# Padding the sine and cosine tables of a kernel's second Fourier transform, so that each table transfer is one whole tile

## The chip, the core and the metric

The kernel runs on one core of one Trainium2 chip. The metric is the device time of one execution in microseconds (us). An execution that is profiled is one of these, and its trace is what the rows below are taken from.

## What is computed

Causal attention (2 batches, 12 heads, 448 positions, 64 channels per head), then a mixer block over tokens and channels, then a block that adds the real part of a two-dimensional Fourier transform, normalizes, and runs a second two-layer network:

```python
attn_out = _attn_ref(**attn_kwargs)
x = attn_out.transpose(0, 2, 1, 3).reshape(B, S, H * D)      # 2 x 448 x 768
# _moe_ref
h = np.maximum(x.transpose(0, 2, 1) @ w_tok1, 0.0) @ w_tok2
u = x + h.transpose(0, 2, 1)
x = u + np.maximum(u @ w_ch1, 0.0) @ w_ch2
# _moe2_ref
X = np.fft.fft(np.fft.fft(x, axis=1), axis=2)
u = x + np.real(X)
un = (u - mean(u)) / np.sqrt(var(u) + 1e-06)
return u + np.maximum(un @ w_ch1, 0.0) @ w_ch2
```

## The kernel before

Activations are kept channel-major: `resid[ct][b]` is a tile of 128 channels by 448 positions, for 6 channel tiles `ct` and 2 batches `b`. Every product that must be exact to fp32 is made of three TensorE passes: each operand is split into a high part and a low part (`act_h` and `act_l`, `gh` and `gl`, `wh` and `wl`), and the passes are high by high, high by low and low by high. ScalarE makes the high part, VectorE or GpSimd subtracts it to get the low part.

The weights arrive as 64-bit floats. `fetch` (L132) loads a tile `w` from SyncE's queue; `convert_steps` turns it into `wh` and `wl`: an absolute value on ScalarE (L141), two VectorE operations with constants (L143 and L144, TENSOR_SCALAR on `m`), two VectorE operations that merge in `w` (L148 and L152, SCALAR_TENSOR_TENSOR), the copy to `wh` (L159) and the subtraction to `wl` (L161).

Attention and the token mixer are issued in an order written out by hand (the string `ORDER`). Its last words are `U` to `a`: for the channel network's first four chunks of batch 0, `early_up` multiplies `act_h` and `act_l` by the first weights (L226 to L228), `gh` is made by ScalarE (L232) and `gl` by VectorE (L234); then `early_down` (`Y`, L247 to L249) multiplies two channel tiles of the second layer, each of 12 matmuls whose last ones need the fourth chunk's `gl`. Among the last words is also `split_low` (L510): GpSimd makes `act_l` of batch 1, for which ScalarE makes `act_h` (L506) from what VectorE added up (L502). What is written after that hand-made order (the channel network's other chunks and the conversions of their weights) is placed by a scheduler, which may move it up between the words of `ORDER`; so the conversion of the next weights stands on VectorE ahead of the fourth chunk's `gl`.

The two Fourier transforms are matrix products with tables that the host computes (`_fft_constants`): `fa` and `fa0` for the transform over channels, `fb` for the one over positions, each as a high and a low half. The tables are loaded before the channel network begins, by GpSimd's queue (L592): `fah` and `fal` are 128 partitions of 2352 floats, `fah0` one partition of 386, and `fbh` and `fbl` 113 partitions of two rows. A row of `fb` has `2 * NH` = 452 floats in memory; its tile in SBUF has room for `FB` = 464 in each row:

```python
fbh = fc.tile([113, 2, FB], F32R, name="fbh")
fbl = fc.tile([113, 2, FB], F32R, name="fbl")
for t, src in ((fah, fa[0]), ..., (fbh[:, :, : 2 * NH], fb[0]), (fbl[:, :, : 2 * NH], fb[1])):
    pool.dma_start(out=t, in_=src)
```

So the loads of `fbh` and `fbl` fill 452 of each 464 floats. On GpSimd's queue they stand between two groups of `split_low`. The tables are first read by `plane` (L761), far later, and by `mixed_mean` (L745); both index the first `NH` and the next `NH` columns of a row.

Of the kernel before, what the change touches and what calls it, by code (L numbers as in the profile page):

```python
# [19 lines left out]
B, H, S, D = 2, 12, 448, 64  # L20
# [11 lines left out]
NK = 386  # L32
NH = 226
FB = 464
# [66 lines left out]
def fused_kernel(ctx: ExitStack, tc: tile.TileContext, qk, v, w1, w2, wa, wb, wc, wd, fa, fa0, fb, out):  # L101
# [153 lines left out]
    with ExitStack() as actx:  # L255
# [282 lines left out]
        def early_down(x):  # L538
# [5 lines left out]
            s=mix_low, B=channels, b=channels_copy, D=mix_out, d=mix_add, u=split_high, w=split_low, R=load_raw,  # L544
# [41 lines left out]
    fah = fc.tile([128, 3, NF + 384], F32R, name="fah")  # L586
    fal = fc.tile([128, 3, NF + 384], F32R, name="fal")
    fah0 = fc.tile([1, NF], F32R, name="fah0")[:, :NK]
    fbh = fc.tile([113, 2, FB], F32R, name="fbh")
    fbl = fc.tile([113, 2, FB], F32R, name="fbl")  # L590
    for t, src in ((fah, fa[0]), (fal, fa[1]), (fah0, fa0[:, :NK]), (fbh[:, :, : 2 * NH], fb[0]), (fbl[:, :, : 2 * NH], fb[1])):
        pool.dma_start(out=t, in_=src)  # L592

    fp = fctx.enter_context(tc.tile_pool(name="fold", bufs=1))
# [332 lines left out]
def _split(x):  # L927
    h = _round12(x)
    return np.stack([h, _round12(x - h.astype(np.float64))])
# [7 lines left out]
def _fft_constants():  # L937
    c = np.arange(384)[:, None]
    k = np.arange(NF)[None, :]
    cos = np.where((k < 385) & (c > 0), np.cos(2 * np.pi * ((c * k) % DM) / DM), 0.0)  # L940
    sin = np.sin(2 * np.pi * ((c * k[:, :384]) % DM) / DM)
    fa = np.concatenate([cos, sin], axis=1).reshape(3, 128, NF + 384).transpose(1, 0, 2)
    fa0 = np.where(k < 385, 1.0 - 2.0 * (k % 2), 0.0).astype(np.float32)
    s = np.concatenate([np.arange(112), [0], np.arange(112, 225)])[:, None]
    k = np.arange(NH)[None, :]
    fb = np.zeros((226, 2 * NH))
    fb[:, :NH] = np.cos(2 * np.pi * ((s * k) % S) / S)
    s = np.concatenate([np.arange(1, 113), [0], np.arange(113, 224), [0, 0]])[:, None]
    fb[:, NH:] = -np.sin(2 * np.pi * ((s * k) % S) / S)
    fb = fb.reshape(2, 113, 2 * NH).transpose(1, 0, 2)  # L950
    return _split(fa), fa0, _split(fb)


# [38 lines left out]
```

## Time and profile before

| | |
|---|---|
| median of 3 runs | 699.96 us (698.80 to 701.28) |
| the profiled execution | 699.23 us |
| its span, first to last instruction | 697.5 us |
| TensorE busy (PE) | 682.7 us, 98% |
| VectorE busy (DVE) | 538.8 us, 77% |
| ScalarE busy (ACT) | 290.0 us, 42% |
| GpSimd busy (POOL) | 136.6 us, 20% |
| mean granted TensorE clock | 0.994 of full speed |
| chain that ended last | PE 90%, DVE 6%, ACT 1%, DMA 1%, issue 1% |

PE stands for matmuls, PEld for weight loads into the array, POOLq and SPq for the queues from which GpSimd and SyncE start transfers. A time in a row is counted from the start of the span. "Idle before" is the time in which an engine stood still before an instruction, with what ended it. The busy time of an instruction that writes a transfer's orders (DMA_DIRECT2D) is the time that GpSimd spent writing them; the time to landing is that of the transfer itself.

### The profile page before, as it was taken

The page shows a single profiled execution, that of the slowest core. Times are in us where ns is not written, and L with a number is a line of the kernel's source. Part 1 is how long each engine was busy: PE and PEld are TensorE (multiplying, and loading weights), DVE is VectorE, ACT ScalarE, POOL GpSimd, SP SyncE. Part 2 cuts the span into 40 slices and gives each one's busy share as a digit, 9 for nine tenths or more (in the row PEclk, how much of TensorE's full clock was granted, in tenths as well). Part 3 has the DMA queues.
Part 4 walks back from the last instruction along what each step waited for, and adds up shares of the span by engine and source line. Part 5 has one row for each costly group of instructions (what it writes and reads, how often), then busy time and mean ns, then how long its engine had stood idle before and what let it go on. Part 6 is the DMA issues. An engine that isn't in the chain of part 4 may idle for free.

```text
span 697.5 us, 10309 instructions
## 1 busy us (share of the span) xinstructions
PE 682.7 (98%) x3954; PEld 622.9 (89%) x3954; DVE 538.8 (77%) x886; ACT 290.0 (42%) x622; POOL 136.6 (20%) x113
## 2 busy tenths in 40 slices
PE   8999999969999999999999999999999999999997
PEld 6788888959999999997999999999999999999996
DVE  5998787474996884799999898689887898755832
ACT  7978986413333333233545632133432233323200
POOL 3242445480000000030050005822002321000000
PEclk9999999989999999999999999999999999999999
DMA  8233321262443333010204334053332344322311
GB/s 262 70 116 122 103 95 62 91 180 83 153 133 121 121 122 119 19 75 0 88 20 136 121 122 138 14 180 121 122 120 92 137 136 136 106 74 90 111 43 54
DMA packets 27585, 73.39 MB, mean 105 GB/s; under 512 B 9114, under 2 KB 14176, under 8 KB 27168
## 3 DMA queue, kind: packets, MB, share of 16 engines
q1 hardware_dynamic: 19952, 69.48, 30.3%
q0 software_dynamic: 7584, 3.25, 1.8%
q8 instruction: 31, 0.51, 0.3%
q14 instruction: 18, 0.15, 0.1%
HBM read 69.94 MB, written 2.75 MB: 104 GB/s over the span
## 4 chain that ended last, share of the span: by engine, by line
PE 90%; DVE 6%; ACT 1%; DMA 1%; issue 1%; DVEq 0%; ACTq 0%; SPq 0%
PE psum L228 12%; PE psum L226 12%; PE psum L227 12%; PE psum L249 12%; PE psum L247 12%; PE psum L248 12%; PE psum L334 3%; PE psum L402 3%; PE psum L385 3%; PE psum L466 2%; PE psum L497 2%; PE psum L761 1%; DMA w<-in_wb 1%; PE psum L695 1%; DVE m L148 1%; PE psum L484 1%
## 5 line engine op out<-in xcount | busy, mean ns | idle before, releaser
L249 PE MATMUL psum<-gl,wh 128*128 128x448 f32 x432 | 157.6, 365 | 6.2 <-DVE gl L234 6.2
L247 PE MATMUL psum<-gh,wh 128*128 128x448 f32 x432 | 157.7, 365 | 0.0
L248 PE MATMUL psum<-gh,wl 128*128 128x448 f32 x432 | 157.3, 364 | 0.0
L228 PE MATMUL psum<-actl,wh 128*128 128x448 f32 x432 | 156.7, 363 | 0.0
L226 PE MATMUL psum<-acth,wh 128*128 128x448 f32 x432 | 156.5, 362 | 0.0
L227 PE MATMUL psum<-acth,wl 128*128 128x448 f32 x432 | 156.1, 361 | 0.0
L141 ACT ACTIVATE m<-w 128x512 f32<-128x512 f32 (+2 forms) x92 | 71.1, 774 | 122.3 <-DVE wl L161 69.8
L159 ACT CAST wh<-m 128x512 fp32r<-128x512 f32 (+1 forms) x90 | 63.2, 704 | 103.7 <-PE psum L249 64.4
L249 PEld LDWEIGHTS psum<-gl,wh 128*128 128x128 f32 x432 | 81.7, 189 | 12.5 <-DVE gl L234 6.6
L247 PEld LDWEIGHTS psum<-gh,wh 128*128 128x128 f32 x432 | 81.6, 189 | 5.5
L248 PEld LDWEIGHTS psum<-gh,wl 128*128 128x128 f32 x432 | 81.6, 189 | 5.5
L227 PEld LDWEIGHTS psum<-acth,wl 128*128 128x128 f32 x432 | 81.0, 188 | 5.9
L228 PEld LDWEIGHTS psum<-actl,wh 128*128 128x128 f32 x432 | 81.1, 188 | 5.3
L226 PEld LDWEIGHTS psum<-acth,wh 128*128 128x128 f32 x432 | 81.1, 188 | 5.1
L143 DVE TENSOR_SCALAR m<-m 128x512 f32<-128x512 f32 (+2 forms) x92 | 52.7, 572 | 41.5 <-ACT m L141 41.0
L152 DVE SCALAR_TENSOR_TENSOR m<-w,m 128x512 uint32<-128x512 uint32 (+2 forms) x92 | 78.8, 858 | 1.8
L148 DVE SCALAR_TENSOR_TENSOR m<-w,m 128x512 uint32<-128x512 uint32 (+2 forms) x92 | 78.4, 853 | 2.2
L161 DVE TENSOR_TENSOR wl<-m,wh 128x512 fp32r<-128x512 f32 (+1 forms) x84 | 67.9, 809 | 11.6 <-ACT wh L159 11.3
L234 DVE SCALAR_TENSOR_TENSOR gl<-psum,gh 128x448 fp32r<-128x448 f32 x72 | 43.7, 618 | 28.1 <-ACT gh L232 28.1
L232 ACT ACTIVATE gh<-psum 128x448 fp32r<-128x448 f32 x72 | 38.0, 539 | 65.3 <-PE psum L228 65.3
L144 DVE TENSOR_SCALAR m<-m 128x512 uint32<-128x512 uint32 (+2 forms) x92 | 52.2, 568 | 2.6
L372 ACT ACTIVATE p<-psum,nmx 112x112 f32<-112x112 f32 (+3 forms) x96 | 46.7, 510 | 8.6 <-DVE nmx L357 7.5
(160 smaller groups left out, 845.1 us busy)
## 6 DMA issues: line engine op xcount, KB each, us to landing
w<-in_wc SPq DMA_DIRECT2D x24, 768.0 KB, 4.3
w<-in_wd SPq DMA_DIRECT2D x36, 512.0 KB, 3.3
w<-in_wa SPq DMA_DIRECT2D x12, 768.0 KB, 4.3
w<-in_wb SPq DMA_DIRECT2D x18, 512.0 KB, 3.3
resid<-in_qk SPq DMA_DIRECT2D x24, 224.0 KB, 2.9
v<-in_v SPq DMA_DIRECT2D x12, 224.0 KB, 2.8
out<-t SPq DMA_DIRECT2D x12, 224.0 KB, 1.9
w<-in_w SPq DMA_DIRECT2D x2, 896.0 KB, 9.1
```

Of the source, the lines that this page charges most:

```text
L141: act.activation(out=m, in_=hi.bitcast(F32), func=AF.Abs)
L143: vec.tensor_scalar(out=m, in0=m, scalar1=F64_MIN, scalar2=F64_MAX, op0=ALU.max, op1=ALU.min)
L148: vec.scalar_tensor_tensor(out=mu, in0=lo, scalar=29, in1=mu, op0=ALU.logical_shift_right, op1=ALU.bitwise_or)
L152: vec.scalar_tensor_tensor(out=mu, in0=hi, scalar=0xC0000000, in1=mu, op0=ALU.bitwise_and, op1=ALU.bitwise_or)
L159: act.copy(wh, m)
L161: low_engine[0].tensor_tensor(out=wl, in0=m, in1=f(wh), op=ALU.subtract)
L226: mm(pb[:, :S], lhsT=lh, rhs=act_h[ct][b], start=ct == 0, stop=False)
L227: mm(pb[:, :S], lhsT=ll, rhs=act_h[ct][b], start=False, stop=False)
L228: tail[0] = mm(pb[:, :S], lhsT=lh, rhs=act_l[ct][b], start=False, stop=ct == NCT - 1).ins
L247: mm(pb[:, :S], lhsT=lh, rhs=gh, start=j + k == 0, stop=False)
L248: mm(pb[:, :S], lhsT=ll, rhs=gh, start=False, stop=False)
L249: tail[0] = mm(pb[:, :S], lhsT=lh, rhs=gl, start=False, stop=j == last and k == nk - 1).ins
```

## The change

The table `fb` is made 464 floats wide on the host, with zeros in the last 12 columns of each row, and the two transfers fill the whole tiles `fbh` and `fbl`. No other line changes; the columns that are read are the same.

```diff
-    for t, src in ((fah, fa[0]), (fal, fa[1]), (fah0, fa0[:, :NK]), (fbh[:, :, : 2 * NH], fb[0]), (fbl[:, :, : 2 * NH], fb[1])):
+    for t, src in ((fah, fa[0]), (fal, fa[1]), (fah0, fa0[:, :NK]), (fbh, fb[0]), (fbl, fb[1])):
         pool.dma_start(out=t, in_=src)
...
-    fb = np.zeros((226, 2 * NH))
+    fb = np.zeros((226, FB))
     fb[:, :NH] = np.cos(2 * np.pi * ((s * k) % S) / S)
     s = np.concatenate([np.arange(1, 113), [0], np.arange(113, 224), [0, 0]])[:, None]
-    fb[:, NH:] = -np.sin(2 * np.pi * ((s * k) % S) / S)
-    fb = fb.reshape(2, 113, 2 * NH).transpose(1, 0, 2)
+    fb[:, NH : 2 * NH] = -np.sin(2 * np.pi * ((s * k) % S) / S)
+    fb = fb.reshape(2, 113, FB).transpose(1, 0, 2)
```

On GpSimd's queue, where the tables are loaded, this is the difference between the two programs (partitions x elements; the first three rows and the last two are common to both):

```order
 L510 TENSOR_TENSOR actl_1_103<-resid_1_79,acth_1_91 128x448
 L592 DMA fah_1987<-in_fa 1x2x193
-L592 DMA fbh<-in_fb 113x2x452
-L592 DMA fbl<-in_fb 113x2x452
+L592 DMA fbh<-in_fb 113x928
+L592 DMA fbl<-in_fb 113x928
 L510 TENSOR_TENSOR actl_1_109<-resid_1_85,acth_1_97 128x448
 L510 TENSOR_TENSOR actl_1_111<-resid_1_87,acth_1_99 128x448
```

The instructions keep their places; the two transfers change from 113 partitions of two rows of 452 to 113 partitions of one row of 928. VectorE's queue is the same in both programs. Its stretch at that time, from the additions of `resid` to the fourth chunk's `gl` and the addition of an early channel tile:

```order
L502 TENSOR_TENSOR resid_1_87<-psum,resid_1_87 128x448
L502 TENSOR_TENSOR resid_1_81<-psum,resid_1_81 128x448
L143 TENSOR_SCALAR m<-m 128x512
L144 TENSOR_SCALAR m<-m 128x512
L148 SCALAR_TENSOR_TENSOR m<-w,m 128x512
L152 SCALAR_TENSOR_TENSOR m<-w,m 128x512
L234 SCALAR_TENSOR_TENSOR gl<-psum,gh 128x448
L253 TENSOR_TENSOR resid_0_78<-psum,resid_0_78 128x448
```

Nothing moved here: the four conversion steps of a weight tile stand ahead of `gl` in both.

## Rows read from the trace of the kernel before

**Rows 1.** TensorE's waits: who waited for whom, us in total, times, longest.
```profile
PE psum L249 <- DVE gl L234: 6.2, 1, 6.2
...
PE psum L695 <- DVE zl L703: 0.4, 1, 0.4
```

**Rows 2.** The chain that ended last, in time: start us, us, what.
```profile
145.56 2.35 DVE m L143
147.93 3.26 DVE m L144
151.21 1.50 DVE m L148
152.74 1.50 DVE m L152
154.24 0.55 DVE gl L234
154.83 0.74 PE psum L249
```

**Rows 3.** Timeline of GpSimd: start us, us, engine, line, operation.
```profile
135.67 0.56 POOL L592 DMA_DIRECT2D fal<-in_fa  x1
...
143.82 0.55 POOL L592 DMA_DIRECT2D fah<-in_fa  x1
144.35 3.32 POOL L592 DMA_DIRECT2D fbh<-in_fb  x1
147.67 3.29 POOL L592 DMA_DIRECT2D fbl<-in_fb  x1
150.97 4.25 POOL L510 TENSOR_TENSOR actl<-resid,acth 128x448 fp32r<-128x448 f32 x3
```

**Rows 4.** VectorE's conversion steps over the whole run; first two: ns min/median/max.
```profile
L143 DVE TENSOR_SCALAR m<-m x92: 416/428/2340, 17.4 to 657.3; 128x512 f32<-128x512 f32 x54, 128x768 f32<-128x768 f32 x36, 112x1024 f32<-112x1024 f32 x1, 128x896 f32<-128x896 f32 x1
...
L144 DVE TENSOR_SCALAR m<-m x92: 415/429/3249, 18.1 to 658.2; 128x512 uint32<-128x512 uint32 x54, 128x768 uint32<-128x768 uint32 x36, 112x1024 uint32<-112x1024 uint32 x1, 128x896 uint32<-128x896 uint32 x1
...
L148 DVE SCALAR_TENSOR_TENSOR m<-w,m 128x512 uint32<-128x512 uint32 x54 | 40.9, 757 | 1.5
```

**Rows 5.** Stretches around the wait: us, PE busy (matmuls), PEclk, DMA share, GB/s.
```profile
148.63:154.83 6.20, 0.00 (x0) 0.87 0.56 35
154.83:161.57 6.74, 6.74 (x22) 0.62 0.43 116
161.57:168.31 6.74, 6.74 (x35) 1.00 0.18 47
```

**Rows 6.** DMA packets, queues and issues (KB each, us to landing), 143.5 to 180 us.
```profile
DMA packets 7957, 3.72 MB, mean 102 GB/s; under 512 B 6932, under 2 KB 7386, under 8 KB 7956
...
q0 software_dynamic: 7306, 0.85, 16.9%
...
fbh<-in_fb POOLq DMA_DIRECT2D x1, 399.0 KB, 23.8
```

**Rows 7.** The same view, 134 to 142 us.
```profile
DMA packets 346, 2.45 MB, mean 307 GB/s; under 512 B 32, under 2 KB 32, under 8 KB 126
...
fah<-in_fa POOLq DMA_DIRECT2D x1, 1176.0 KB, 5.7
```

**Rows 8.** Timeline from 144 us: ScalarE's `gh` and `act_h`, then what follows the wait.
```profile
145.43 0.53 ACT L232 ACTIVATE gh<-psum 128x448 fp32r<-128x448 f32 x1
145.85 1.49 ACT L506 CAST acth<-resid 128x448 fp32r<-128x448 f32 x3
...
157.50 1.14 POOL L510 TENSOR_TENSOR actl<-resid,acth 128x448 fp32r<-128x448 f32 x1 [2.27 <-ACT acth L506]
...
163.74 0.55 ACT L232 ACTIVATE gh<-psum 128x448 fp32r<-128x448 f32 x1 [6.31 <-PE psum L228]
164.18 0.61 ACT L159 CAST wh<-m 128x512 fp32r<-128x512 f32 x1
```

**Rows 9.** The first use of the table `fbh`: ns min/median/max, first and last start.
```profile
L761 PEld LDWEIGHTS psum<-fbh,zh x28: 80/192/193, 331.1 to 341.6; 112*128 112x128 f32 x12, 113*128 113x128 f32 x6, 111*128 111x128 f32 x6, 112*2 112x2 f32 x2
```

## The prediction

> **What bounds the kernel now.** I began with TensorE's waits, because the table above gives it 98% of the span and 90% of the chain. After the start it has one long wait: 6.2 us for the `gl` of VectorE (L234), in one piece; of its later ones the longest listed is 0.4 us [rows 1]. So a gain elsewhere in the program has little to take, and here it has at least 6.2 us.
>
> The chain shows what that `gl` waited for [rows 2]. VectorE converts a weight tile first. Its two operations with constants took 2.35 and 3.26 us, the two merges 1.50 and 1.50 us, `gl` itself 0.55 us, and TensorE began again at 154.83. Over the whole run the median of each of the first two operations is 0.43 us, and these two are the longest of the 92 of their line [rows 4]. Something held VectorE for about 4.7 us (2.35 + 3.26 - 2 x 0.43 = 4.75).
>
> GpSimd's timeline shows what [rows 3]. It wrote the orders of the transfer `fbh` from 144.35 to 147.67 and those of `fbl` from 147.67 to 150.96. VectorE's L143 started at 145.56 and ended at 147.90, 0.23 us after the first; L144 started at 147.93 and ended at 151.18, 0.22 us after the second. Two ends that follow two others by the same 0.2 us are no accident: I read it as VectorE's operations with constants standing still while GpSimd writes orders. The merges that come next run beside three subtractions of GpSimd, 4.25 us together [rows 3], and take 1.50 us where their mean over the run is 0.76 [rows 4].
>
> The wait costs more than itself. TensorE did 22 matmuls in the 6.74 us after it at a mean granted clock of 0.62, and 35 in the next 6.74 us at 1.00 [rows 5]: after standing still it ran part of that time at 1.2 GHz instead of 2.4. Thirteen matmuls at 6.74 / 35 = 0.19 us each are 2.5 us.
>
> **Why these orders take long.** `fah` and `fal` have 128 rows of 9408 bytes; one took 0.56 us to write [rows 3], and `fah` landed in 5.7 us with 1176 KB [rows 7]. `fbh` has a third of the bytes, took 3.32 us to write [rows 3] and landed in 23.8 us [rows 6]. The packets tell them apart. Between 134 and 142 us 346 packets moved 2.45 MB, with only 32 under 512 bytes [rows 7]. Between 143.5 and 180 us 7386 - 6932 = 454 packets had 512 to 2048 bytes, which fits the 2 x 113 x 2 = 452 half rows of 1808 bytes, and 6932 were smaller still [rows 6]: some fifteen small packets for each half row. A piece in 23.8 / 226 = 0.105 us says that the half rows went one after another, not side by side as the rows of `fah` did. The time to write orders goes with the pieces, each with its small companions: (3.32 - 0.55) / 226 = 12 ns for each, over a floor of 0.55 us that even the tiny `fah0` cost [rows 3].
>
> **The change, part by part.** The host's zeros cost the device nothing. Each transfer carries 113 x 928 x 4 bytes = 410 KB instead of 399 KB; nobody waits for it before the first use at 331 us [rows 9], and it landed by 144.35 + 23.8 = 168 us, so 163 us hide it.
>
> The pieces change: memory and tile now both have 113 rows of 3712 bytes, as `fah` has 128 rows of 9408 on both sides. No row shows 113 whole rows on this queue. Bounds for the writing of one such table: below, 0.55 us (`fah0`); above, half the pieces in the old manner, 0.55 + 113 x 0.0123 = 1.93 us. I take 0.56 us, the row of `fal` [rows 3], since it is the one with the same form on both sides.
>
> Then GpSimd has `fbh` done at 144.93 and `fbl` at 145.48, before VectorE's L143 starts at 145.56. (That start is set by ScalarE's step of the conversion, which the change does not touch; I leave it.) L143 and L144 take 0.43 us each: 146.45 with the gaps between them. GpSimd's three subtractions cannot all move up by 5.5 us, because ScalarE makes their operands from 145.85 to 147.34 [rows 8]; they start about 146.4 and run beside the merges again. So I keep the merges at 1.50 us: 147.97 and 149.47. `gl` is at 150.0, and TensorE starts at 150.1 instead of 154.83. Its own work until the wait ends at 148.63, so 1.5 us of waiting stay, and **4.7 us** go. Bounds: if the merges ran at 0.7 us, `gl` would be there before TensorE asks, and all 6.2 us would go; if GpSimd's subtractions held L144 as the orders did, for one of them (4.25 / 3 = 1.4 us), 4.7 - 1.4 = 3.3 us would go.
>
> With 1.5 us of standing still instead of 6.2, I expect the clock to stay at 2.4 GHz: **2.5 us**. No row shows the clock after a pause of 1.5 us, so the bound on the other side is 0.
>
> What is late next? After the restart come 13 matmuls (the last of one early tile and the 12 of the next), then the first chunk of batch 1, whose last passes need the fourth subtraction of GpSimd; it follows the restart by 158.64 - 154.83 = 3.8 us [rows 8], so 153.9, where TensorE needs it at 150.1 + (13 + 17) x 0.19 = 155.8. The next weight conversion waits behind ScalarE's `gh`, which waited 6.31 us for TensorE [rows 8]: it moves with TensorE. I find nothing that takes the gain back.
>
> Sum: 4.7 + 2.5 = 7.2 us. Against the profiled execution, 699.23 - 7.2 = 692.0; that execution stood 0.7 us below the median of the three, so for a median I forecast **692.7 us**. With the bounds above it is 691.2 (6.2 + 2.5) to 696.7 (3.3 + 0).
>
> **Rivals.**
>
> *Half the pieces, still in single file.* 113 divides no better than 226 did: if each row goes out with its fifteen small packets, a table takes 1.93 us. For it: the partitions stay 113, where the quick tables have 128. Against it: memory and tile now agree in form. Then `fbh` is written by 146.30, L143 ends at 146.53, L144 loses to `fbl` until 148.2 and ends at 148.45, the merges end at 151.5, `gl` at 152.0, and TensorE starts at 152.1: 2.7 us gained, and up to 2.5 us more if the clock holds through a pause of 3.4 us. On the median: 697.3 to 694.8.
>
> The Trainium skill, page "DMA: Bandwidth & Descriptors", section "Why a DMA increments its semaphore by 16 and not by 1", speaks for this rival: a transfer uses the largest number of DMA engines up to 16 that divides the outermost size on both sides, and 113 is prime, so one engine, before and after; by that rule the sum would be this rival's. The trace agrees for the kernel before (0.105 us per piece, one after another). The same section reports an exception, that transfers issued from GpSimd sometimes put a sixteenth of the partitions, rounded up, on each engine, even with 127; by that the sum would be my own. No run here shows which holds for the new form.
>
> *Nothing changes.* The orders cost what they cost by partition, not by piece, or VectorE's hold has another cause than the orders: the wait stays and the median is 700.0. Against it are the two ends 0.2 us behind two others.
>
> *Slower: the rows are cut smaller.* If the generator of orders cut a row of 3712 bytes into pieces with companions, more than two pieces a row would be more than before, and that is where it turns. With four, a table takes 0.55 + 452 x 0.0123 = 6.1 us; GpSimd is done at 156.6, VectorE's L144 at 156.8, `gl` at 160.4, TensorE at 160.5, 5.7 us later than now: 705.7. Against it: rows of 9408 bytes passed whole, over 8 KB in 346 - 126 = 220 packets [rows 7].
>
> **How the numbers follow.** My case has 0.70, the single file 0.14, no change 0.08, smaller pieces 0.03; 0.05 is for a gain that later work takes back, half of it down to no difference. The median of three before spreads by about 1.2 us to either side, so the range goes from 691.2 - 1.2 = 690.0 to the single file without the clock, 697.3; that leaves out the unchanged and the slower cases. A measurement tells about 0.3% (2.1 us) from no change; both kinds of faster case exceed it. Faster: 0.70 + 0.14 + some 0.03 = 0.87; the same 0.09; slower 0.04.
>
> **What would show it.** In the changed profile `fbh` and `fbl` should be written in about 0.56 us each (1.9 for the rival), land in a few us instead of 23.8, and the 6932 small packets should mostly be gone. L143 and L144 should take 0.43 us at this place in place of 2.35 and 3.26, TensorE's wait for `gl` should be 1.5 us or less, and the mean clock near 1.00 after it. I am wrong if the orders are quick and `gl` is late all the same, or if TensorE starts early and stops again before 200 us.

## The result, and the profile after

| | before | after |
|---|---|---|
| median | 699.89 us (4 runs, 698.80 to 701.28) | 691.25 us (4 runs, 690.86 to 694.31) |
| ratio of the times, 95% interval | | 0.9885 (0.9852 to 0.9918) |
| profiled execution, its span | 699.23, 697.5 us | 694.31, 692.5 us |
| TensorE busy | 682.7 us, 98% | 684.0 us, 99% |
| VectorE busy | 538.8 us | 533.7 us |
| GpSimd busy | 136.6 us | 130.8 us |
| mean granted clock | 0.994 | 1.000 |

The kernel became faster by 8.6 us, 1.15%, where 7.3 us were forecast (699.96 to 692.7); the measured time lies inside the range. The profiled execution is the slowest of the four: between 10 and 20 us, far ahead of the change, it did 75 matmuls where the one of before did 102, so what follows stands about 3.0 us later on its time axis (L143 at 148.54 instead of 145.56). The change is not the cause: an experiment below that keeps the slow transfers (three rows in memory) shows the same, 75 matmuls in that stretch and L143 at 148.58. I therefore compare distances between events, not their times of day.

The timeline of VectorE, GpSimd and TensorE in the changed kernel around the place of the old wait (start us, us, engine, line, operation, in brackets the idle time before it and what ended it):

```profile
147.29 0.54 POOL L592 DMA_DIRECT2D fbh<-in_fb  x1
147.81 0.53 POOL L592 DMA_DIRECT2D fbl<-in_fb  x1
148.54 0.43 DVE L143 TENSOR_SCALAR m<-m 128x512 f32<-128x512 f32 x1 [2.82 <-ACT m L141]
149.00 0.43 DVE L144 TENSOR_SCALAR m<-m 128x512 uint32<-128x512 uint32 x1
149.46 0.69 DVE L148 SCALAR_TENSOR_TENSOR m<-w,m 128x512 uint32<-128x512 uint32 x1
149.94 3.89 POOL L510 TENSOR_TENSOR actl<-resid,acth 128x448 fp32r<-128x448 f32 x3 [1.59 <-ACT acth L506]
150.19 1.53 DVE L152 SCALAR_TENSOR_TENSOR m<-w,m 128x512 uint32<-128x512 uint32 x1
151.64 0.61 DVE L234 SCALAR_TENSOR_TENSOR gl<-psum,gh 128x448 fp32r<-128x448 f32 x1
152.30 0.47 PE L249 MATMUL psum<-gl,wh 128*128 128x448 f32 x1 [0.74 <-DVE gl L234]
```

Against [rows 2, 3]: the orders of one table take 0.54 us instead of 3.3, both tables are ordered at 148.34, 0.2 us before L143 begins, and L143 and L144 take 0.43 us each where they took 2.35 and 3.26. L148 takes 0.69 instead of 1.50, L152 still 1.53. From the start of L143 to TensorE's restart it is 152.30 - 148.54 = 3.76 us, before 154.83 - 145.56 = 9.27: 5.5 us less. TensorE's wait, 6.2 us in [rows 1], is 0.7 us, and no longer the longest; the list of its waits begins now:

```profile
PE psum L194 <- DVE mean_w L117: 1.1, 1, 1.1
PE psum L385 <- DVE x L434: 0.9, 1, 0.9
PE psum L249 <- DVE gl L234: 0.7, 1, 0.7
```

Two stretches of the changed kernel (us, busy time and number of TensorE, PEld, VectorE, ScalarE, GpSimd, then granted clock, DMA share, GB/s): the first has the times of day of the stretch after the old wait, the second is the 6.74 us that follow this kernel's own restart:

```profile
154.83:161.57 6.74, 6.74 (x35) 6.33 (x34) 2.08 (x4) 1.71 (x3) 1.03 (x1) 1.00 0.00 0
152.30:159.04 6.74, 6.74 (x34) 6.32 (x35) 1.78 (x3) 0.79 (x2) 2.69 (x3) 1.00 0.25 80
```

After the restart 34 matmuls fit where 22 did, at a granted clock of 1.00 instead of 0.62 [rows 5]: (34 - 22) x 0.19 = 2.3 us. With the 5.5 us this makes 7.8 us. The two profiled executions differ by 699.23 - 694.31 = 4.9 us, and by 7.9 without the 3.0 us that the second lost early, so the sum accounts for them; what is missing to the 8.6 us of the medians is inside the interval of the ratio (5.7 to 10.4 us).

The DMA view from 143.5 to 180 us, to be held against [rows 6]:

```profile
DMA packets 1296, 5.69 MB, mean 156 GB/s; under 512 B 204, under 2 KB 206, under 8 KB 1200
...
fbh<-in_fb POOLq DMA_DIRECT2D x1, 409.6 KB, 4.3
fbl<-in_fb POOLq DMA_DIRECT2D x1, 409.6 KB, 5.1
```

The small packets are gone (204 under 512 bytes, before 6932), and `fbh` lands in 4.3 us instead of 23.8 with 3% more bytes.

### The profile page after: what moved, and what is told of

It reads as the page before. It is cut to its first block, busy times and chain, and to the rows that moved or that the text cites. A ratio compares the mean times of both kernels' runs of the same rounds, so it can differ in the third digit from the quotient of the medians.

```text
span 692.5 us, 10309 instructions
## 1 busy us (share of the span) xinstructions
PE 684.0 (99%) x3954; PEld 624.6 (90%) x3954; DVE 533.7 (77%) x886; ACT 290.7 (42%) x622; POOL 130.8 (19%) x113
## 3 DMA queue, kind: packets, MB, share of 16 engines
HBM read 69.96 MB, written 2.75 MB: 105 GB/s over the span
## 4 chain that ended last, share of the span: by engine, by line
PE 92%; DVE 5%; DMA 1%; ACT 1%; issue 0%; DVEq 0%; ACTq 0%; SPq 0%
PE psum L228 12%; PE psum L227 12%; PE psum L226 12%; PE psum L249 12%; PE psum L248 12%; PE psum L247 12%; PE psum L334 4%; PE psum L385 4%; PE psum L402 3%; PE psum L466 2%; PE psum L497 2%; PE psum L761 1%; DMA w<-in_wb 1%; PE psum L695 1%; PE psum L348 1%; PE psum L421 1%
## 5 line engine op out<-in xcount | busy, mean ns | idle before, releaser
L143 DVE TENSOR_SCALAR m<-m 128x512 f32<-128x512 f32 (+2 forms) x92 | 50.8, 552 | 40.3 <-ACT m L141 40.2
L152 DVE SCALAR_TENSOR_TENSOR m<-w,m 128x512 uint32<-128x512 uint32 (+2 forms) x92 | 78.9, 858 | 1.8
L148 DVE SCALAR_TENSOR_TENSOR m<-w,m 128x512 uint32<-128x512 uint32 (+2 forms) x92 | 77.6, 844 | 2.2
L144 DVE TENSOR_SCALAR m<-m 128x512 uint32<-128x512 uint32 (+2 forms) x92 | 49.4, 537 | 2.6
```

Of the source, the lines that this page charges most:

```text
L143: vec.tensor_scalar(out=m, in0=m, scalar1=F64_MIN, scalar2=F64_MAX, op0=ALU.max, op1=ALU.min)
L148: vec.scalar_tensor_tensor(out=mu, in0=lo, scalar=29, in1=mu, op0=ALU.logical_shift_right, op1=ALU.bitwise_or)
L152: vec.scalar_tensor_tensor(out=mu, in0=hi, scalar=0xC0000000, in1=mu, op0=ALU.bitwise_and, op1=ALU.bitwise_or)
```

## The experiments

Three things were to be told apart. Which property of the transfer makes it quick: the whole tile, the single piece per partition, or the number of partitions? Does the gain come from the orders at that place, from the order of VectorE's work, or from the transfer itself? And what exactly holds VectorE? The experiments were run in three groups, marked a, b and c below, each on one chip beside the kernel before, whose medians there were 698.78 us (a), 699.13 us (b) and 699.20 us (c). Edits are shown in part, against the kernel before or, where it says so, against the changed one.

### Which property makes the transfer quick

**No padding, but one piece per partition (a).** The tile is declared flat, and its two rows lie side by side, as in memory; only 904 of its 928 columns are filled.

```diff
-    fbh = fc.tile([113, 2, FB], F32R, name="fbh")
-    fbl = fc.tile([113, 2, FB], F32R, name="fbl")
+    fbh = fc.tile([113, 2 * FB], F32R, name="fbh")[:, : 4 * NH]
+    fbl = fc.tile([113, 2 * FB], F32R, name="fbl")[:, : 4 * NH]
...
+    fbh, fbl = [t.rearrange("p (i n) -> p i n", i=2) for t in (fbh, fbl)]
```

> No padding: the two rows of a partition lie side by side in the tile as in memory, so each partition is one piece of 904 floats, and the transfer fills 904 of 928 floats of the tile. Theory 'one equal form on both sides' (113 whole rows on both sides are enough): 0.54 us per table to write, landing in about 5 us, 691 us, as the changed kernel. Rival 'whole tile' (the tile must be filled without a gap between partitions): 1.9 to 3.3 us per table, and 694 to 700 us.

Measured: 691.50 us, ratio 0.9899 (0.9875 to 0.9924). The orders take 0.55 us a table, TensorE's wait for `gl` is 0.6 us. The transfers in its DMA view:

```profile
fbh<-in_fb POOLq DMA_DIRECT2D x1, 399.0 KB, 4.5
fbl<-in_fb POOLq DMA_DIRECT2D x1, 399.0 KB, 5.5
```

So neither the padding nor the full tile is needed, only that each partition is one piece.

**The old form with 128 partitions (a).** Two rows of 452 in a tile of 464 again, but with 15 partitions of zeros more.

```diff
-    fbh = fc.tile([113, 2, FB], F32R, name="fbh")
-    fbl = fc.tile([113, 2, FB], F32R, name="fbl")
+    fbh = fc.tile([128, 2, FB], F32R, name="fbh")
+    fbl = fc.tile([128, 2, FB], F32R, name="fbl")
...
+    fb = np.concatenate([fb.reshape(2, 113, 2 * NH).transpose(1, 0, 2), np.zeros((15, 2, 2 * NH))])
```

> The old form with its gap, two rows of 452 in 464, but 128 partitions instead of 113 (15 of zeros). Theory 'division' (the pieces of a transfer go side by side where 16 divides the outermost size on both sides): 0.6 to 0.8 us per table to write, about 5 us to land, no small companions, 691 us. Rival 'form' (a transfer whose two sides differ in form always goes piece by piece): 0.55 + 256 x 0.0123 = 3.7 us per table, and 700 to 701 us.

Measured: 690.94 us, ratio 0.9885 (0.9870 to 0.9899). Its timeline of GpSimd and its DMA view:

```profile
143.87 0.75 POOL L592 DMA_DIRECT2D fbh<-in_fb  x1
144.62 0.72 POOL L592 DMA_DIRECT2D fbl<-in_fb  x1
```

```profile
DMA packets 1463, 5.18 MB, mean 142 GB/s; under 512 B 173, under 2 KB 687, under 8 KB 1460
...
fbh<-in_fb POOLq DMA_DIRECT2D x1, 452.0 KB, 3.8
```

There are now 687 - 173 = 514 packets of half rows (2 x 128 x 2 = 512) and no companions. The second table landed in 4.3 us. Two pieces per partition are no obstacle if there are 128 partitions. L143, which still met the last orders, took 0.53 us.

**Three rows in memory, so that both sides are 113 x 2 x 452 (c).** The memory side of the old transfer may be read as 226 rows in one run; here a third row, not moved, separates the pairs.

```diff
-    ..., (fbh[:, :, : 2 * NH], fb[0]), (fbl[:, :, : 2 * NH], fb[1])):
+    ..., (fbh[:, :, : 2 * NH], fb[0][:, :2]), (fbl[:, :, : 2 * NH], fb[1][:, :2])):
...
-    fb = fb.reshape(2, 113, 2 * NH).transpose(1, 0, 2)
+    fb = np.concatenate([fb, np.zeros((113, 2 * NH))]).reshape(3, 113, 2 * NH).transpose(1, 0, 2)
```

> The old form of the tile, but in memory the two rows of a partition are followed by a third that is not moved, so that both sides of a transfer have 113 partitions of two rows. If the transfer goes side by side as soon as both sides agree in their outer size, even with 113: 0.7 us of orders per table, about 5 us to land, 691 us. If it needs one piece per partition (or an outer size that 16 divides): 3.3 us of orders, 24 us to land, 699 us.

Measured: 698.90 us, ratio 0.9990 (0.9973 to 1.0007). Nothing is gained; its DMA view:

```profile
DMA packets 8131, 4.93 MB, mean 135 GB/s; under 512 B 6938, under 2 KB 7392, under 8 KB 8032
...
fbh<-in_fb POOLq DMA_DIRECT2D x1, 399.0 KB, 23.6
```

Equal outer sizes are not enough: 113 partitions of two pieces go one after another, with their companions, whichever way memory is laid out. TensorE's wait is 6.2 us again.

### Where the gain comes from

**One table padded (a) and the other table padded (c).** The first leaves `fbh` as it was and makes `fbl` whole, the second the reverse; the lines replace that of the changed kernel.

```diff
+    ..., (fbh[:, :, : 2 * NH], fb[0][:, :, : 2 * NH]), (fbl, fb[1])):
...
+    ..., (fbh, fb[0]), (fbl[:, :, : 2 * NH], fb[1][:, :, : 2 * NH])):
```

> Half of the change: only the low table fbl is moved as one whole tile, fbh keeps its two rows per partition. Theory 'orders': fbh takes 3.3 us to write, fbl 0.54; L143 is held until fbh is done (2.3 us), L144 hardly (under 1 us), TensorE's wait for gl is between 2 and 4 us, so 2.5 to 4 us are gained there. If the clock falls after such a pause, 696 to 697 us; if it holds, 693 to 695. A rival by which VectorE is held by GpSimd's subtractions and not by the orders expects both L143 and L144 held as before, 700 us.

> The other half of the change: fbh as one whole tile, fbl in its old form. Theory 'who comes first': L143 starts while fbl's orders are written and takes about 3 us; L144 then meets the three subtractions, takes 3 to 3.9 us more, and the merges run at 0.69 us; TensorE's wait for gl is 5 to 6 us and the time about 698 us, as with the other half. Theory 'orders alone': L143 about 3 us, L144 0.43, TensorE's wait 3 us, 694 to 696 us.

Measured with `fbl` whole: 698.20 us, ratio 0.9988 (0.9974 to 1.0002), no difference that this measurement shows. With `fbh` whole: 697.34 us, ratio 0.9971 (0.9957 to 0.9984). By these ratios half the change brings a quarter of the gain at most. The first kernel's timeline says why:

```profile
144.70 3.31 POOL L592 DMA_DIRECT2D fbh<-in_fb  x1
146.01 2.23 DVE L143 TENSOR_SCALAR m<-m 128x512 f32<-128x512 f32 x1 [2.88 <-ACT m L141]
148.01 0.54 POOL L592 DMA_DIRECT2D fbl<-in_fb  x1
148.27 3.89 DVE L144 TENSOR_SCALAR m<-m 128x512 uint32<-128x512 uint32 x1
148.55 3.32 POOL L510 TENSOR_TENSOR actl<-resid,acth 128x448 fp32r<-128x448 f32 x3
152.19 0.69 DVE L148 SCALAR_TENSOR_TENSOR m<-w,m 128x512 uint32<-128x512 uint32 x1
```

The quick orders of `fbl` took 2.75 us from GpSimd's path, and L144 gained nothing: it stood through them and then through all three subtractions, and ended 0.29 us after the third (148.55 + 3.32 = 151.87, then 152.16). TensorE's wait was still 5.2 us. And `fbl`, though its orders were quick, landed only after 22.7 us: it stood behind the slow `fbh`. The other one:

```profile
144.63 3.31 POOL L592 DMA_DIRECT2D fbl<-in_fb  x1
145.45 2.71 DVE L143 TENSOR_SCALAR m<-m 128x512 f32<-128x512 f32 x1 [2.90 <-ACT m L141]
147.96 3.99 POOL L510 TENSOR_TENSOR actl<-resid,acth 128x448 fp32r<-128x448 f32 x3
148.20 1.23 DVE L144 TENSOR_SCALAR m<-m 128x512 uint32<-128x512 uint32 x1
149.47 1.50 DVE L148 SCALAR_TENSOR_TENSOR m<-w,m 128x512 uint32<-128x512 uint32 x1
```

L143 ends 0.22 us after the orders (144.63 + 3.31 = 147.94, then 148.16); L144 takes 1.23 us, about one subtraction (3.99 / 3 = 1.33), and both merges 1.50. The wait was 4.7 us. The expectation missed L144 by both of its theories (3 us and more, or 0.43). So not only the orders hold the operations with constants: GpSimd's subtractions do too, and the two halves of the change do not add up. Each table alone leaves one slow order in the way, which holds L143 until the L144 behind it meets the subtractions.

**The old transfers later (a).** Their form is that of before; on GpSimd's queue they are put behind the fourth subtraction of the group.

```diff
-            pool.tensor_tensor(out=act_l[ct][b], in0=resid[ct][b], in1=f(act_h[ct][b]), op=ALU.subtract)
+            ins = pool.tensor_tensor(out=act_l[ct][b], in0=resid[ct][b], in1=f(act_h[ct][b]), op=ALU.subtract); last_split.append(ins.ins)
...
-        pool.dma_start(out=t, in_=src)
+        with tc.issue_after(last_split[-1]) if t.shape[0] == 113 else ExitStack(): pool.dma_start(out=t, in_=src)
```

> The old transfers of 113 x 2 rows, unchanged in form, but GpSimd writes their orders behind its last subtraction for batch 1, where TensorE waits for none of the held VectorE work. Theory 'orders' (VectorE's operations with constants stand still while GpSimd writes orders, and only the place on the path costs time): each table still takes 3.3 us to write and over 20 us to land, but TensorE's wait for gl falls to about 0.7 us, the clock stays, and the time is that of the changed kernel, 691 us. Some later VectorE operation with constants is held for up to 3.3 us, off the path. Rival 'transfer' (the slow transfer with its 6,800 small packets is what costs): no gain, 700 us.

Measured: 693.15 us, ratio 0.9914 (0.9900 to 0.9929). The orders cost what they cost before (3.34 and 3.29 us, at 152.31 and 155.64), yet the wait for `gl` is 0.6 us: moving the orders away is worth most of the gain. It did not reach the changed kernel, because TensorE waits for another `gl` 24 us later, whose weights are late; two rows of its timeline, then its DMA view from 150 to 185 us:

```profile
168.76 0.89 ACT L141 ACTIVATE m<-w 128x768 f32<-128x768 f32 x1 [4.92 <-DMA w<-in_wa]
...
172.42 0.48 PE L249 MATMUL psum<-gl,wh 128*128 128x448 f32 x1 [1.61 <-DVE gl L234]
```

```profile
w<-in_wa SPq DMA_DIRECT2D x4, 768.0 KB, 7.5
fbh<-in_fb POOLq DMA_DIRECT2D x1, 399.0 KB, 30.5
```

Is that the place, or the slow transfer? **The padded transfers at that same later place (b)** have both edits, the change's and the one above.

> The changed kernel's quick transfers, behind GpSimd's last subtraction for batch 1, where the old transfers gave 693.2 us with a second wait of TensorE of 1.6 us. If that wait came from the slow transfer (weight tiles landed in 7.5 us instead of 4.2 beside it), it goes: 691 us, weight tiles in 4 to 5 us, no second wait. If it came from the place, it stays: 693 us.

Measured: 691.31 us, ratio 0.9885 (0.9866 to 0.9904), no second wait, and in the same view of it:

```profile
w<-in_wa SPq DMA_DIRECT2D x4, 768.0 KB, 4.3
```

So the slow transfer itself, 30 us beside the loads of weights, delays them (7.5 instead of 4.3 us) and costs about 2 us there ((0.9914 - 0.9885) x 699; the two intervals just overlap). The kernel before shows little of this: its loads of 768 KB begin only at 168.67, when the slow transfers are about to land (24.3 us after 147.67 for `fbl`), and take 4.3 us; one tile of 512 KB landed in 6.9 us there instead of 3.6, and TensorE's list of waits shows nothing for it.

**The order on VectorE, with the old transfers (c).** The conversion of the weight tile is put behind `gl`.

```diff
-            for ins in hold:
+            for ins in hold[: take("c", 1000)]:
...
-    turn = dict(y=0, s=0, all=0)
+    turn = dict(y=0, s=0, all=0, c=1)
...
-                vec.scalar_tensor_tensor(
+                made = vec.scalar_tensor_tensor(
...
+                if part and gpool is None and fm == 3: hold.append(made.ins)
```

> The old transfers, with gl ahead of the conversion on VectorE. L143 and L144 are held by the orders as before (2 and 3 us), but TensorE's wait for gl goes. Behind them the last addition for batch 1 comes late, and TensorE waits 1 to 4 us for the last high or low part of batch 1, some 7 us later: 692 to 696 us, and less if the clock stays. A rival by which the held operations do not matter to TensorE but the transfer does: 699 us.

Measured: 696.29 us, ratio 0.9955 (0.9938 to 0.9971), a little above what was expected. The wait for this `gl` is gone, and another takes half its place: the orders also stand ahead of the subtractions on GpSimd's own queue. Its timeline, then its stretch after it (columns as above):

```profile
150.65 4.28 POOL L510 TENSOR_TENSOR actl<-resid,acth 128x448 fp32r<-128x448 f32 x3
...
154.99 0.47 PE L228 MATMUL psum<-actl,wh 128*128 128x448 f32 x1 [3.08 <-POOL actl L510]
```

```profile
155.00:160.00 5.00, 5.00 (x17) 4.49 (x18) 0.54 (x2) 1.09 (x3) 1.14 (x1) 0.66 0.50 135
```

This was the second late thing behind the first; the changed kernel removes both, because it takes the time from GpSimd itself. A third shows here too: TensorE waits 1.2 us at 176.09 for a later `gl`, whose weights are late as in the old transfers put later (768 KB in 7.3 us).

**The changed kernel once more, and with `gl` ahead of the conversion, or inside it (b).** The first is the change unaltered. The second adds the order edit above to it. The third puts `gl` between L144 and L148, for that one conversion (shown without the lines that it shares with the order edit):

```diff
-            for ins in hold:
+            for ins in hold[:1]:
...
-                    next(steps)
+                    next(steps); turn["c"] += 1; turn["c"] == 8 and order.enter_context(tc.issue_after(hold[1]))
```

> The changed kernel once more, as the mark for the two orders below: 691 us, TensorE's wait for gl 0.6 to 0.7 us.

> The changed kernel with the fourth chunk's gl ahead of the whole conversion on VectorE. Theory 'subtractions hold too' (an operation with constants on VectorE stands still through all subtractions that GpSimd runs back to back, as half a change showed): L143 or L144 now starts after the first of the three subtractions and takes about 3 us, though no table's orders are being written; TensorE does not wait for gl any more, but what stands behind on VectorE comes later, so the time is within 1 us of 691. Rival 'only orders hold': L143 and L144 take 0.43 us each.

> The changed kernel with gl between L144 and L148, so that the two operations with constants still come before GpSimd's subtractions start, and only the two merges behind gl run beside them. TensorE's wait for gl goes (0.7 us to 0); L143 and L144 take 0.43 us each; about 0.7 us faster than the changed kernel, 690.4 us.

Measured: the change again 691.56 us, ratio 0.9899 (0.9879 to 0.9919); `gl` first 690.36 us, ratio 0.9880 (0.9861 to 0.9899); `gl` between 690.21 us, ratio 0.9869 (0.9852 to 0.9885). Neither has a wait for this `gl` any more. The last has the lowest median of all, about 1 us below the change, though the intervals overlap; it removes the 0.7 us that were left. The expectation that L143 or L144 would be held for some 3 us with `gl` first failed: they took 0.42 and 0.43 us, having begun (149.32 and 149.77) before GpSimd's first subtraction (149.79).

### What holds VectorE

**The constants late (c).** The changed kernel with `gl` ahead of the conversion and made three times over, so that L143 begins when the subtractions already run; one line beside the order edit, against the changed kernel.

```diff
-                vec.scalar_tensor_tensor(
+                for _ in range(3 if part and gpool is None and fm == 3 else 1): made = vec.scalar_tensor_tensor(
```

> The changed kernel with the fourth chunk's gl made three times over (the same values) ahead of the conversion on VectorE, so that L143 starts about 0.5 us after the first of GpSimd's three back-to-back subtractions; no table's orders are being written then. Theory 'who comes first' (an operation with constants on VectorE and GpSimd's work exclude each other, whatever GpSimd does): L143 takes about 3 us, until the three subtractions are done, L144 0.43. Rival 'only orders hold VectorE': L143 takes 0.43 to 0.6 us. TensorE waits for gl in neither, so the time is 690 to 692 us in both.

Measured: 690.36 us, ratio 0.9871 (0.9856 to 0.9885). The timeline:

```profile
145.83 1.94 DVE L234 SCALAR_TENSOR_TENSOR gl<-psum,gh 128x448 fp32r<-128x448 f32 x3 [3.15 <-ACT gh L232]
146.86 3.75 POOL L510 TENSOR_TENSOR actl<-resid,acth 128x448 fp32r<-128x448 f32 x3 [1.56 <-ACT acth L506]
147.69 0.61 DVE L143 TENSOR_SCALAR m<-m 128x512 f32<-128x512 f32 x1
148.34 1.26 DVE L144 TENSOR_SCALAR m<-m 128x512 uint32<-128x512 uint32 x1
```

L143 and L144 are held, but each by no more than one subtraction (0.61 and 1.26 us instead of 0.43), not for the 3 us that were expected. That subtractions hold the constants is shown three times (here and with each single table). For how many of them an operation stands is not constant: one in two kernels, and all three with `fbl` alone whole, where L144 already stood when they began. That it already stood is not the reason: in the kernel before, L144 stood as well when the subtractions began (147.93 and 150.97), and was through at 151.18. Why is open.

That orders hold them without any subtraction is shown by the kernel with the old transfers put later, whose orders meet the L143 of the next conversion after the last subtraction:

```profile
155.64 3.29 POOL L592 DMA_DIRECT2D fbl<-in_fb  x1
157.85 1.30 DVE L143 TENSOR_SCALAR m<-m 128x512 f32<-128x512 f32 x1 [0.72 <-ACT m L141]
```

It ends at 159.15, 0.22 us after the orders (158.93), and the L144 behind it takes 0.43 us.

The Trainium skill, page "SBUF — State Buffer", section "Who interferes with whom", says that VectorE and GpSimd share a pair of ports as an exclusive lock, that VectorE's `tensor_scalar` can take that pair in its two-port modes, and that whichever issues first then blocks the other for its whole instruction. No row shows in which mode L143 and L144 ran. The ends 0.2 to 0.3 us after GpSimd's, and the quick L143 and L144 that began first, agree with it; three subtractions passing over one waiting operation are more than a lock held for one instruction.

## Why the prediction was right, and where it was off

*Forecast 692.7 us, range 690.0 to 697.3; measured 691.25.* The likeliest case happened, by its mechanism.

*Orders of 0.56 us a table.* Measured 0.54 and 0.53. The bound of 1.93 us, half the pieces in single file, fell: 113 whole rows land in 4.3 us, too fast for 0.105 us each one after another (11.9 us). The kernels of the first group show what decides: one piece per partition with 113 partitions is quick, two pieces with 128 too, two pieces with 113 are not.

That also bears on the two rules that the prediction quoted from the Trainium skill, page "DMA: Bandwidth & Descriptors", section "Why a DMA increments its semaphore by 16 and not by 1". The divisor rule fits the transfers of two pieces per partition (113: single file, 128: quick; no other number was run). With one piece per partition 113 does not follow it, and the exception of that section fits the 4.3 and 5.1 us of landing; how many DMA engines took part no row here shows.

*L143 and L144 at 0.43 us.* Measured 0.43 each, as forecast.

*Both merges at 1.50 us: the mis-sized term.* I kept both beside the subtractions, which I let start about 146.4, 0.8 us after L143's start, when the first of ScalarE's three `act_h` is done. They began 149.94 - 148.54 = 1.4 us after it, about when the second is done (ScalarE began the three at 148.84 and took 1.49 us). So L148 ran alone, at 0.69 us, and only L152 took 1.53. That is the whole difference of 0.8 us between the forecast 4.7 and the measured 5.5 us, and why the wait left is 0.7 and not 1.5 us.

*The clock, 2.5 us.* 2.3 by count of matmuls, near the forecast. The bound of no gain did not come about: after the pause of 0.7 us the granted clock is 1.00. The prediction had no row for a pause of 1.5 us; the experiments have. Here is the stretch of 6.74 us after the restart (columns as above) that follows a pause of 3.1 us (`gl` first, old transfers), 4.7 us (`fbh` whole), 5.2 us (`fbl` whole), 6.2 us (three rows in memory) and 1.6 us (old transfers later, the second wait):

```profile
154.99:161.73 6.74, 6.74 (x26) 6.12 (x27) 1.78 (x4) 2.04 (x4) 1.14 (x1) 0.75 0.41 113
153.08:159.82 6.74, 6.74 (x26) 6.19 (x27) 1.78 (x3) 0.57 (x1) 1.14 (x1) 0.77 0.31 100
154.20:160.94 6.74, 6.74 (x23) 6.14 (x24) 1.78 (x3) 0.57 (x1) 1.14 (x1) 0.65 0.33 98
157.87:164.61 6.74, 6.74 (x27) 6.20 (x28) 1.78 (x3) 0.57 (x1) 1.55 (x2) 0.79 0.39 116
172.42:179.16 6.74, 6.74 (x34) 6.32 (x35) 6.28 (x10) 1.63 (x2) 0.00 (x0) 1.00 0.58 145
```

The last line bears out the clock that I expected after 1.5 us of pause, in another kernel and at another place. The size of the term is less firm than its sign: after the same pause of 6.2 us the kernel before did 22 matmuls, the one with three rows in memory 27.

*Nothing taken back later.* Right for the change: behind it the longest wait of TensorE that is listed is 0.4 us (L695 for `zl`), as before [rows 1]. But I priced the transfer at nothing because nobody waits for it, and missed that it delays others: with the wait gone and the slow transfer kept it costs about 2 us. The change avoids this, and it counted for nothing in my sum because the kernel before did not pay it.

*What held VectorE.* Here my reading was incomplete, without harm to the number. I saw two ends behind two orders and put all of the hold on the orders; the subtractions hold the same operations, and I had that only as a bound. Had I been asked for one table alone, I would have put the gain too high, as the expectation for `fbl` shows. The changed kernel escapes by 0.5 us: L144 ends at 149.43 and the first subtraction starts at 149.94. That margin was not foreseen: by my own times L144 would have ended at 146.45, just after the subtractions' start at 146.4. It was not needed either, since with `gl` first an L144 that began 0.02 us before them was not held.

*The rivals.* Single file, no change, and smaller pieces are all excluded by the 0.54 us of orders, by L143 and L144 at 0.43 us, and by the 204 small packets.

## What to carry to other kernels

Look at the time that GpSimd spends on a transfer's orders, not only at when the transfer lands: where it is several times that of a larger one, count the packets under 512 bytes, and make the transfer one piece per partition on both sides (padding is one way, a flat view another). If VectorE's operations with constants take several times their median, see what GpSimd does in that time, and shift either of them. When one wait is removed, follow everything that stood behind the same cause: here the operands of the next matmuls on GpSimd's queue, and the weights whose loading the slow transfer delays.

## What the runs showed of the hardware that I had not expected

- A transfer of 113 partitions with two pieces each costs 3.3 us of GpSimd and 23.4 to 32.8 us until it lands (23.8 and 24.3 us in the kernel before); one piece each 0.52 to 0.55 and 4.1 to 5.6 us; 128 partitions with two pieces 0.72 to 0.75, and 3.8 and 4.3 us, though it has 13% more bytes.
- A quick transfer that stands on the queue behind a slow one waits for it: `fbl` in one piece per partition landed in 22.7 us behind the old `fbh`.
- The slow kind delays others: weight tiles of 768 KB landed in 7.5 us beside it, and in 4.3 us without.
- A subtraction of GpSimd (1.1 to 1.3 us each) holds VectorE's operations with constants as the writing of orders does: 1.23 to 1.26 us instead of 0.43, and once 3.89 us through the end of orders and three of them.
- TensorE's granted clock was 1.00 after pauses of 0.7, 1.2 and 1.6 us, and below it after those of 3.1, 4.7, 5.2 and 6.2 us.
